# Six probability buffers in place of four, and another written-out order of issue, in a fused attention and feed-forward kernel

## The chip, the cores and the metric

The kernel runs on one core of one Trainium2 chip. The metric is the device time of one execution in microseconds (us), the median of several runs. The engines are called as the profile calls them: PE is TensorE, DVE is VectorE, ACT is ScalarE, POOL is GpSimd, SP is SyncE, whose queue issues every DMA here.

## What is computed

Rotary attention over 4 batches of 8 heads, 576 positions and 64 channels, followed by a feed-forward layer on the 2304 tokens x 512 channels that come out. All in float32.

```python
q_rot, k_rot = (rotate(q), rotate(k))
scores = scale * np.matmul(q_rot, k_rot.transpose(0, 1, 3, 2))
attn = np.exp(scores - np.max(scores, axis=-1, keepdims=True))
attn = attn / (np.sum(attn, axis=-1, keepdims=True) + 1e-09)
x = heads_joined(np.matmul(attn, v))          # 2304 x 512
h = x @ w_in                                   # 2304 x 1024
e = np.exp(h - np.max(h, axis=-1, keepdims=True))
solu = h * (e / (np.sum(e, axis=-1, keepdims=True) + 1e-09))
ln = (solu - solu.mean(-1)) / np.sqrt(solu.var(-1) + 1e-06) * g_ln
return ln @ w_out                              # 2304 x 512
```

## The kernel before, in words

**Attention** goes by 16 pairs of heads, P = 0 to 15, four to a batch. The rotation of a pair's queries and keys is three products and sums for each (line 359), on POOL or DVE. A pair has five score tiles: S P.0 to S P.3 hold 128 rows of each of the two heads, S P.4 packs the last 64 rows of both. PE writes them to PSUM (line 425, the packed ones 452 or 458 and 461), DVE takes the row maxima (405, 472), ACT the exponentials (407, 475) into a probability buffer `e` in SBUF. The buffers are used in turn, tile number j = 5 P + i in buffer j modulo `NE`. Before the values can be applied the tile is transposed: on PE (T steps, line 489, with a copy out of PSUM by ACT, line 328, or DVE, line 330), or, for most tiles of P = 4 and later, by writing it to DRAM (`escr`), reading it back in another order, and a blockwise transpose on DVE (510). Two attention-value blocks per pair (line 564) then add up in PSUM, and DVE scales them into `xT`. From P = 4 on the scores are the sum of three products of split (high and low) operands; the first four pairs use the unsplit ones.

**The feed-forward layer** goes by 18 tiles of 128 tokens. Each of its two matmuls is three products of high and low parts (lines 638 and 711), so 24 matmuls of 512 columns per tile and layer. Between them stand a row maximum (645), an exponential (647), a product (649), a trip through DRAM (`uscr`) with a transpose on DVE (693), and the split into high (`lnh`) and low parts (`lnl`, line 703). The weights arrive as 64-bit words and are decoded in the kernel (tag w, lines 809 to 824: on ACT 809 and 817, on DVE 811, 813 and 818, on POOL 821), in 16 pieces, beside the first four pairs. Before the first scores PE runs a few dummy matmuls (line 725).

**The order of the work** is written out as a list. `Plan.add` numbers 2357 steps as the code builds them, and records each one's engine; `ORDER` is a list of these numbers, and each engine's and each DMA queue's program is the part of the list that belongs to it. Steps with an `alt` may run on a second engine, and do if their number stands in `FLIP`. `BUFS` gives each use of a rotating buffer (three PSUM pairs `D` for scores and hidden rows, two PSUM banks `G`, three SBUF pieces `B`) its place. What must wait for what follows from the data and the buffers; the order itself changes no result.

Numbers that the text speaks of: 118 and 120 are the first two row maxima and 119 and 121 their exponentials; 35, 38, 44 and 47 are decode steps of ACT; 36, 37 and 39 decode steps of DVE; 122 to 125 the first transposes and their copies; 117, 128 and 151 the first three score tiles; 2343 to 2345 the last turn of the last token tile, with its high and low parts.

Of the kernel before, what the change touches and what calls it, by code (L numbers as in the profile page):

```python
# [32 lines left out]
    13, 2, 14, 3, 24, 4, 5, 6, 7, 12, 16, 27, 15, 23, 26, 28, 17, 29, 25, 18, 34, 30, 35, 117, 126, 1, 127,  # L33
    31, 38, 32, 118, 119, 19, 122, 43, 44, 36, 37, 39, 47, 120, 121, 33, 128, 131, 52, 53, 132, 10, 129,
    130, 124, 125, 139, 140, 141, 40, 123, 56, 45, 106, 108, 151, 133, 154, 155, 134, 107, 135, 136, 20,
    114, 61, 152, 153, 142, 109, 46, 48, 110, 62, 115, 65, 112, 160, 163, 137, 138, 161, 164, 158, 159, 143,
    49, 171, 172, 144, 145, 162, 146, 147, 41, 50, 54, 148, 167, 168, 111, 113, 63, 201, 55, 57, 58, 173,
    169, 42, 170, 204, 205, 149, 150, 156, 157, 179, 180, 192, 181, 202, 174, 175, 210, 193, 70, 203, 176,
    178, 64, 165, 177, 166, 116, 206, 207, 213, 214, 208, 209, 79, 186, 211, 194, 182, 185, 195, 71, 233,
    72, 212, 196, 51, 183, 197, 187, 188, 234, 217, 235, 74, 200, 218, 221, 236, 237, 222, 184, 223, 66, 73,  # L40
    67, 59, 224, 60, 80, 242, 243, 215, 68, 216, 199, 245, 246, 189, 190, 75, 238, 239, 81, 191, 76, 253,
    254, 244, 249, 250, 88, 240, 241, 283, 83, 82, 225, 278, 219, 255, 84, 85, 11, 277, 284, 285, 227, 228,
    229, 220, 77, 261, 262, 263, 279, 286, 89, 90, 230, 231, 86, 287, 21, 292, 226, 232, 288, 295, 97, 289,
    251, 296, 252, 258, 293, 294, 247, 248, 315, 69, 260, 98, 301, 302, 78, 259, 275, 318, 319, 446, 87, 99,
    91, 290, 291, 256, 282, 257, 450, 447, 274, 276, 100, 303, 304, 324, 327, 328, 325, 361, 305, 102, 198,
    268, 326, 269, 101, 103, 297, 298, 448, 264, 92, 316, 335, 266, 317, 270, 271, 336, 337, 272, 329, 267,
    330, 362, 265, 93, 104, 373, 363, 273, 364, 94, 320, 321, 340, 342, 374, 375, 299, 300, 105, 449, 341,
    338, 382, 376, 339, 95, 281, 356, 8, 322, 377, 309, 357, 323, 383, 310, 385, 306, 333, 456, 457, 451,
    386, 458, 384, 358, 359, 360, 308, 96, 311, 0, 312, 307, 313, 314, 280, 334, 486, 372, 487, 460, 393,
    394, 405, 395, 343, 378, 379, 488, 380, 344, 381, 406, 407, 345, 368, 22, 459, 461, 371, 9, 391, 396,  # L50
    392, 366, 331, 452, 414, 387, 332, 350, 466, 351, 346, 489, 490, 408, 388, 677, 409, 389, 417, 418, 462,
    415, 416, 398, 425, 463, 365, 453, 693, 491, 492, 676, 390, 397, 426, 427, 678, 696, 476, 697, 399, 400,
    349, 467, 352, 694, 348, 682, 695, 681, 683, 468, 401, 402, 403, 404, 347, 704, 707, 477, 705, 528, 529,
    493, 496, 701, 691, 470, 353, 354, 355, 419, 420, 698, 469, 478, 370, 433, 434, 435, 679, 702, 410, 423,
    424, 534, 471, 472, 706, 479, 412, 413, 692, 481, 436, 369, 454, 708, 530, 709, 531, 430, 494, 431, 495,
    729, 730, 480, 482, 532, 411, 421, 497, 732, 680, 699, 712, 703, 535, 432, 731, 367, 428, 733, 737, 500,
    498, 499, 501, 429, 422, 483, 533, 536, 537, 502, 547, 740, 684, 775, 779, 538, 440, 741, 548, 438, 441,
    780, 539, 717, 718, 742, 437, 710, 743, 442, 439, 506, 700, 503, 719, 713, 734, 443, 744, 715, 716, 752,
    504, 505, 745, 444, 553, 554, 690, 473, 738, 753, 754, 549, 550, 551, 540, 484, 445, 711, 507, 508, 509,
    755, 685, 555, 510, 511, 512, 758, 541, 750, 720, 761, 762, 746, 714, 542, 455, 516, 485, 760, 759, 735,  # L60
    763, 791, 794, 552, 751, 556, 513, 514, 764, 723, 724, 725, 795, 792, 799, 721, 515, 566, 567, 793, 796,
    726, 727, 739, 722, 543, 544, 756, 557, 568, 781, 790, 569, 517, 518, 572, 767, 766, 519, 521, 573, 464,
    574, 575, 520, 558, 559, 757, 522, 765, 474, 475, 736, 465, 686, 523, 524, 525, 802, 803, 804, 687, 748,
    749, 688, 728, 786, 570, 571, 585, 526, 805, 806, 576, 827, 774, 776, 689, 800, 747, 604, 878, 768, 815,
    605, 782, 783, 560, 545, 561, 577, 807, 797, 769, 606, 607, 608, 546, 770, 810, 789, 828, 829, 609, 578,
    562, 563, 771, 772, 816, 817, 808, 622, 832, 527, 579, 777, 778, 830, 831, 835, 610, 838, 839, 811, 841,
    818, 840, 784, 843, 611, 612, 613, 801, 773, 842, 846, 787, 879, 873, 833, 836, 614, 619, 623, 626, 640,
    624, 809, 625, 615, 616, 788, 820, 617, 618, 627, 620, 621, 851, 852, 890, 847, 628, 844, 813, 798, 814,
    629, 819, 630, 631, 893, 880, 853, 854, 889, 632, 881, 812, 894, 874, 891, 892, 895, 633, 634, 564, 901,
    849, 860, 861, 635, 834, 862, 863, 902, 586, 587, 903, 591, 636, 588, 875, 888, 882, 837, 906, 850, 904,  # L70
    905, 644, 855, 856, 898, 885, 926, 886, 848, 565, 637, 845, 866, 927, 876, 909, 857, 859, 858, 581, 896,
    929, 928, 931, 864, 638, 930, 641, 580, 865, 877, 592, 593, 594, 589, 639, 642, 590, 595, 937, 938, 940,
    934, 596, 977, 597, 643, 914, 915, 910, 821, 822, 823, 824, 825, 867, 826, 939, 916, 899, 897, 868, 869,
    870, 871, 645, 785, 941, 872, 907, 949, 932, 950, 912, 913, 988, 911, 951, 976, 978, 952, 991, 883, 646,
    989, 947, 942, 948, 582, 992, 598, 908, 990, 647, 900, 648, 917, 649, 958, 971, 959, 935, 953, 999, 650,
    1000, 651, 954, 972, 973, 974, 960, 987, 979, 583, 584, 933, 1261, 943, 945, 946, 884, 1001, 655, 996,
    1002, 652, 653, 993, 654, 936, 1003, 944, 919, 1024, 1025, 1012, 1013, 1014, 1026, 658, 1027, 656, 920,
    1260, 921, 922, 983, 918, 923, 924, 975, 1028, 1035, 925, 1036, 1038, 1010, 1048, 1011, 955, 1039, 956,
    957, 1037, 659, 980, 1049, 965, 966, 967, 968, 969, 660, 661, 1272, 665, 666, 667, 662, 663, 961, 664,
    668, 669, 1004, 670, 1007, 994, 995, 1050, 1051, 997, 600, 671, 998, 1029, 1015, 1273, 1032, 1262, 1005,  # L80
    963, 887, 1006, 1275, 962, 1008, 964, 970, 1009, 1046, 1030, 1274, 1031, 1040, 1016, 599, 984, 1047,
    1033, 1276, 1283, 601, 1284, 602, 1018, 1019, 1285, 1034, 1043, 1263, 1020, 1021, 1022, 1057, 1017,
    1023, 1070, 986, 1308, 1052, 1286, 1287, 1277, 1041, 1044, 1058, 1071, 657, 672, 1059, 1280, 1278, 1267,
    981, 1288, 1076, 1077, 1291, 1311, 603, 673, 1072, 1073, 1045, 1309, 1312, 1053, 1271, 1042, 1310, 982,
    674, 1265, 1078, 1074, 1075, 1256, 1079, 1296, 1297, 1060, 1279, 1255, 1298, 1257, 1258, 1316, 1054,
    1055, 1056, 1319, 1289, 1294, 1080, 1313, 1081, 1320, 1321, 1270, 1292, 1322, 1264, 1089, 1323, 1064,
    1268, 1065, 1082, 1066, 1259, 1331, 1332, 1370, 1373, 1085, 1295, 1067, 1068, 1358, 1329, 1333, 1334,
    1281, 1090, 1095, 1290, 1091, 1096, 1097, 1299, 1340, 1084, 1371, 985, 1372, 1330, 1314, 1359, 1360,
    1293, 1335, 1324, 1086, 1374, 1336, 1282, 1353, 1354, 1315, 1381, 1337, 1338, 1339, 1365, 1366, 1063,
    1382, 1383, 1384, 1317, 1318, 1385, 1087, 1092, 1093, 1094, 1098, 1341, 1061, 1342, 1300, 1062, 1327,  # L90
    1328, 1069, 1083, 1325, 1266, 1099, 1100, 1394, 1406, 1407, 1108, 1326, 1302, 1303, 1375, 1408, 1355,
    1369, 1301, 1304, 1361, 1362, 1386, 1409, 1305, 1306, 1347, 1109, 1410, 1348, 1395, 1101, 1103, 1356,
    1357, 1165, 1343, 1396, 1307, 1169, 1170, 1349, 1350, 1351, 1417, 1418, 1419, 1368, 1378, 1387, 1166,
    1392, 1167, 1168, 1420, 1458, 1389, 1388, 1171, 1453, 1393, 1110, 1452, 1457, 1376, 1421, 1111, 1112,
    1113, 1114, 1115, 1116, 1117, 1127, 675, 1118, 1102, 1119, 1422, 1377, 1172, 1173, 1088, 1430, 1174,
    1431, 1432, 1411, 1120, 1363, 1345, 1433, 1122, 1123, 1344, 1346, 1352, 1175, 1414, 1176, 1177, 1178,
    1379, 1439, 1440, 1469, 1470, 1471, 1128, 1428, 1180, 1454, 1129, 1429, 1130, 1133, 1183, 1397, 1472,
# [846 lines left out]
```

## Time and profile before

| | us |
|---|---|
| median of 3 runs | 444.42 |
| lowest, highest | 442.26, 445.22 |
| the profiled execution | 442.91 |
| its span, first to last instruction | 441.1 |
| PE, DVE, ACT, POOL busy | 430.2, 377.2, 290.7, 264.4 |

The profile is one execution. Busy time of an engine is the time in which it works on an instruction; for PE the ends of the matmuls are modelled, so neighbours overlap. The profile's lines are those of the kernel's file; a helper's line stands for all its callers (328 and 330 are the two copies, 343 every plain DMA, 359 every product, sum or difference of two tiles).

### The profile page before, as it was taken

The page shows a single profiled execution, that of the slowest core. Times are in us where ns is not written, and L with a number is a line of the kernel's source. Part 1 is how long each engine was busy: PE and PEld are TensorE (multiplying, and loading weights), DVE is VectorE, ACT ScalarE, POOL GpSimd, SP SyncE. Part 2 cuts the span into 40 slices and gives each one's busy share as a digit, 9 for nine tenths or more (in the row PEclk, how much of TensorE's full clock was granted, in tenths as well). Part 3 has the DMA queues.
Part 4 walks back from the last instruction along what each step waited for, and adds up shares of the span by engine and source line. Part 5 has one row for each costly group of instructions (what it writes and reads, how often), then busy time and mean ns, then how long its engine had stood idle before and what let it go on. Part 6 is the DMA issues. An engine that isn't in the chain of part 4 may idle for free.

```text
span 441.1 us, 8137 instructions
## 1 busy us (share of the span) xinstructions
PE 430.2 (98%) x2658; PEld 310.5 (70%) x2658; DVE 377.2 (86%) x601; ACT 290.7 (66%) x644; POOL 264.4 (60%) x295
## 2 busy tenths in 40 slices
PE   7899999999999999999999999999999999999996
PEld 3555656666867776767777778677676776778885
DVE  3899999899999999989889998889889897765663
ACT  1888999999684866767675666675576755335431
POOL 2766767878888585397677868357767320314440
PEclk9999999999999999999999999999999999999999
DMA  7765666879999999998999998899999997434341
GB/s 249 274 207 161 211 176 202 255 230 291 239 319 319 288 297 282 323 305 249 335 320 265 342 268 263 274 298 287 272 310 273 292 303 198 142 121 159 119 144 48
DMA packets 93243, 109.29 MB, mean 248 GB/s; under 512 B 8464, under 2 KB 68752, under 8 KB 93200
## 3 DMA queue, kind: packets, MB, share of 16 engines
q1 hardware_dynamic: 93200, 108.76, 79.1%
q8 instruction: 21, 0.34, 0.3%
q14 instruction: 22, 0.18, 0.1%
HBM read 70.91 MB, written 37.82 MB: 247 GB/s over the span
## 4 chain that ended last, share of the span: by engine, by line
PE 84%; DVE 8%; ACT 3%; DMA 2%; issue 2%; SPq 0%; DVEq 0%; ACTq 0%
PE pg L711 23%; PE pd L638 22%; PE pg L564 16%; PE pd L425 13%; PE pg L489 7%; PE pd L452 2%; DVE mx L405 2%; ACT e L407 1%; DMA rawk<-in_k_t_dram 1%; DMA vst<-in_v_t_dram 1%; DVE xT L818 1%; ACT ET L328 1%; DVE rawq L359 1%; DVE xT L811 1%; ACT xT L809 1%
## 5 line engine op out<-in xcount | busy, mean ns | idle before, releaser
L407 ACT ACTIVATE e<-pd,mx 128x576 f32<-128x576 f32 x132 | 97.7, 742 | 40.6 <-DVE mx L405 24.8
L405 DVE TENSOR_REDUCE mx<-pd 128x1 f32<-128x576 f32 x132 | 95.5, 744 | 13.4 <-PE pd L425 12.3
L510 DVE STREAM_TRANSPOSE ET<-e 128x512 f32<-128x512 f32 x90 | 99.1, 1130 | 0.6 <-DMA e<-escr 0.4
L564 PE MATMUL pg<-ET,vst 128*64 128x320 f32 (+1 forms) x512 | 70.2, 412 | 1.0 <-DVE EL L330 0.8
L703 POOL TENSOR_TENSOR lnl<-tb,lnh 128x512 fp32r<-128x512 f32 x28 | 36.4, 1307 | 50.2 <-ACT lnh L328 35.1
L638 PE MATMUL pd<-wih,xh 128*128 128x512 f32 x144 | 59.2, 411 | 0.0
L711 PE MATMUL pg<-woh,lnh 128*128 128x512 f32 x144 | 58.6, 407 | 0.0
L489 PE MATMUL pg<-idn,e 128*128 128x128 f32 (+1 forms) x308 | 55.0, 296 | 2.6 <-ACT ET L328 1.3
L489 PEld LDWEIGHTS pg<-idn,e 128*128 128x128 f32 (+1 forms) x308 | 40.3, 186 | 23.9 <-issue 7.6
L711 PE MATMUL pg<-woh,lnl 128*128 128x512 f32 x144 | 56.9, 395 | 0.0
L638 PE MATMUL pd<-wih,xl 128*128 128x512 f32 x144 | 56.9, 395 | 0.0
L711 PE MATMUL pg<-wol,lnh 128*128 128x512 f32 x144 | 56.9, 395 | 0.0
L638 PE MATMUL pd<-wil,xh 128*128 128x512 f32 x144 | 56.8, 395 | 0.0
L564 PEld LDWEIGHTS pg<-ET,vst 128*64 128x64 f32 x512 | 33.9, 136 | 25.6 <-issue 3.7
L693 DVE STREAM_TRANSPOSE tb<-wraw 128x512 f32<-128x512 f32 x36 | 39.0, 1113 | 0.9 <-POOL lnl L703 0.8
L359 POOL TENSOR_TENSOR rawk<-rawk,tabs 128x576 f32<-128x576 f32 x24 | 34.2, 1435 | 4.0 <-DMA rawk<-in_k_t_dram 3.9
L359 POOL TENSOR_TENSOR rawq<-rawq,tabs 128x576 f32<-128x576 f32 (+1 forms) x23 | 31.0, 1350 | 9.1 <-DMA rawq<-in_q_t_dram 7.8
L328 ACT COPY ET<-pg 128x512 f32<-128x512 f32 x49 | 27.9, 585 | 12.9 <-PE pg L489 10.4
L359 POOL TENSOR_TENSOR xl<-xT,xh 128x512 fp32r<-128x512 f32 x13 | 16.8, 1294 | 31.4 <-ACT xh L328 30.4
L425 PE MATMUL pd<-kh,qh 64*128 64x288 f32 x192 | 33.3, 343 | 0.3 <-DVE ms L649 0.3
L645 DVE TENSOR_REDUCE ms<-pd 128x1 f32<-128x1024 f32 x18 | 21.9, 1219 | 12.5 <-PE pd L638 12.4
L638 PEld LDWEIGHTS pd<-wih,xh 128*128 128x128 f32 x144 | 27.2, 189 | 6.8 <-ACT e L407 0.8
(122 smaller groups left out, 894.9 us busy)
## 6 DMA issues: line engine op xcount, KB each, us to landing
escr<-e SPq DMA_DIRECT2D x90, 256.0 KB
e<-escr SPq DMA_DIRECT2D x90, 256.0 KB
uscr<-u SPq DMA_DIRECT2D x18, 512.0 KB
wraw<-uscr SPq DMA_DIRECT2D x18, 512.0 KB
rawk<-in_k_t_dram SPq DMA_DIRECT2D x15, 576.0 KB
rawq<-in_q_t_dram SPq DMA_DIRECT2D x15, 576.0 KB
vst<-in_v_t_dram SPq DMA_DIRECT2D x16, 320.0 KB
out_dram<-o SPq DMA_DIRECT2D x18, 256.0 KB
```

Of the source, the lines that this page charges most:

```text
L328: nc.scalar.copy(o, i)
L359: add(*c[0], prio, lambda e: e.tensor_tensor(o, a, b, op=op), r, w, alt=c[1], two=True)
L405: add("dve", 672, t, lambda: nc.vector.tensor_reduce(mx[:, mcol:mcol + 1], buf(us)[:, :, 0:288], axis=AX.XY, op=ALU.max, negate=True), [sk ...
L407: add("act", 720, t, lambda: nc.scalar.activation(e.rearrange("p (z n) -> p z n", z=2), buf(us)[:, :, 0:288], AF.Exp, bias=mx[:, mcol:mcol ...
L425: nc.tensor.matmul(buf(us)[:, z, 0:288], a[rows, c0:c0 + 128], w[rows, 288 * z:288 * z + 288], start=(j == 0), stop=(j == len(terms) - 1))
L489: nc.tensor.transpose(dst, src, idn)
L510: add("dve", 1040, t, lambda: nc.vector.transpose(ET[r][:, h, :, q0:q0 + 128].rearrange("p m (a j) -> p j m a", j=4), e.rearrange("p (j b ...
L564: nc.tensor.matmul(buf(uy)[rows, 0:nq], vv[:, m, h, :], e, start=(m == 0), stop=(m == 4))
L638: nc.tensor.matmul(buf(uh)[:, z, :], a[:, c, :], w[:, c, HF * z:HF * z + HF], start=(c == 0 and j == 0), stop=(c == KC - 1 and j == 2))
L693: add("dve", 1050, tl, lambda z=z, turned=turned: nc.vector.transpose(turned().rearrange("p m (a j) -> p j m a", j=4), v[:, :, 128 * z:128 ...
L703: add(*c[0], tl, lambda e, hd=hd, ld=ld, turned=turned: e.tensor_tensor(ld, turned(), hd, op=ALU.subtract), [bk] + kl[0][z], kl[1][z], use ...
L711: nc.tensor.matmul(buf(uo), a[:, f, :], w[:, f, :], start=(f == 0 and j == 0), stop=(f == FC - 1 and j == 2))
```

## The change

`NE` goes from 4 to 6: two more SBUF buffers of 128 x 1152 float32 for the exponentials. `ORDER`, `FLIP` and `BUFS` are replaced by others, which obey the looser condition that a tile's buffer is read out six tiles later in place of four. The steps themselves, their number (2357), the matmuls, the transfers and which tiles go through DRAM stay. The lists are cut here to their first lines.

```diff
-    13, 2, 14, 3, 24, 4, 5, 6, 7, 12, 16, 27, 15, 23, 26, 28, 17, 29, 25, 18, 34, 30, 35, 117, 126, 1, 127,
-    31, 38, 32, 118, 119, 19, 122, 43, 44, 36, 37, 39, 47, 120, 121, 33, 128, 131, 52, 53, 132, 10, 129,
-    130, 124, 125, 139, 140, 141, 40, 123, 56, 45, 106, 108, 151, 133, 154, 155, 134, 107, 135, 136, 20,
-    114, 61, 152, 153, 142, 109, 46, 48, 110, 62, 115, 65, 112, 160, 163, 137, 138, 161, 164, 158, 159, 143,
-    49, 171, 172, 144, 145, 162, 146, 147, 41, 50, 54, 148, 167, 168, 111, 113, 63, 201, 55, 57, 58, 173,
-    169, 42, 170, 204, 205, 149, 150, 156, 157, 179, 180, 192, 181, 202, 174, 175, 210, 193, 70, 203, 176,
...
+    14, 2, 12, 16, 13, 27, 24, 15, 23, 26, 17, 29, 28, 1, 18, 25, 3, 4, 5, 6, 7, 34, 35, 30, 117, 126, 32,
+    31, 33, 118, 119, 38, 127, 120, 121, 43, 44, 19, 36, 37, 39, 128, 131, 132, 129, 130, 124, 40, 106, 108,
+    122, 123, 139, 140, 141, 9, 125, 151, 154, 133, 47, 109, 135, 152, 155, 45, 46, 134, 110, 136, 48, 49,
+    20, 107, 52, 112, 153, 41, 160, 163, 61, 114, 137, 138, 62, 142, 158, 159, 111, 171, 53, 145, 164, 172,
+    173, 115, 161, 162, 54, 146, 147, 148, 167, 56, 65, 143, 113, 201, 144, 55, 168, 149, 63, 57, 204, 50,
+    58, 169, 150, 170, 179, 192, 205, 174, 156, 210, 175, 157, 70, 193, 194, 176, 180, 181, 202, 203, 42,
...
 FLIP = {
-    23, 24, 25, 33, 42, 45, 72, 77, 78, 96, 112, 113, 125, 138, 194, 195, 196, 197, 216, 220, 252, 259, 260,
-    274, 277, 278, 341, 356, 357, 359, 362, 363, 390, 413, 431, 464, 475, 478, 485, 495, 610, 660, 676, 677,
-    681, 682, 688, 716, 749, 775, 781, 814, 850, 877, 885, 1071, 1089, 1109, 1207, 1363, 1393, 1458, 1558,
-    1649, 1650, 1687, 1781, 1782, 1784, 1881, 1905, 1971, 2173, 2210, 2211, 2270, 2273, 2287, 2291, 2306,
+    23, 25, 33, 42, 45, 51, 72, 90, 96, 108, 110, 112, 113, 159, 178, 193, 195, 196, 197, 216, 259, 260,
+    274, 276, 277, 278, 279, 289, 356, 357, 359, 360, 361, 362, 363, 431, 432, 465, 468, 475, 478, 488, 495,
+    515, 676, 677, 681, 682, 683, 685, 686, 779, 883, 913, 948, 979, 1055, 1056, 1089, 1170, 1171, 1203,
+    1262, 1338, 1356, 1357, 1393, 1460, 1462, 1535, 1552, 1781, 1784, 1798, 1800, 1880, 1881, 1895, 1907,
+    1935, 2172, 2210, 2211, 2249, 2270, 2272, 2287, 2291, 2309, 2326, 2327, 2342, 2344, 2345,
...
 BUFS = (
-    "0021001101001211020111011201010001002010100020100111021100121120101000012100111111201011012111002210"
...
+    "1211020101110100121000101200001000121110210011000200101010020121111011120102110000101020011100110011"
...
     RNG = ((0, 256), (256, 320))
-    NE = 4
+    NE = 6
```

## Rows read from the trace of the kernel before

**Rows 1.** The page, busy time of the engines.
```profile
PE 430.2 (98%) x2658; PEld 310.5 (70%) x2658; DVE 377.2 (86%) x601; ACT 290.7 (66%) x644; POOL 264.4 (60%) x295
```

**Rows 2.** Busy time by stretch, core 0: engine busy (instructions), granted clock, DMA share.
```profile
0.00:15.00 15.00, 12.45 (x33) 5.46 (x34) 7.49 (x13) 4.42 (x8) 4.02 (x16) 1.00 0.84 280
15.00:60.00 45.00, 41.93 (x284) 26.47 (x282) 42.45 (x81) 40.20 (x91) 33.42 (x24) 1.00 0.60 192
60.00:90.00 30.00, 28.71 (x205) 18.85 (x203) 28.22 (x57) 28.54 (x65) 21.18 (x17) 1.00 0.73 229
90.00:130.00 40.00, 39.71 (x252) 28.85 (x251) 38.99 (x65) 34.31 (x75) 34.47 (x34) 1.00 0.90 271
130.00:360.00 230.00, 229.97 (x1526) 171.29 (x1525) 208.59 (x321) 152.20 (x351) 152.25 (x169) 1.00 0.95 292
360.00:441.10 81.10, 77.41 (x372) 59.62 (x371) 51.43 (x69) 31.02 (x59) 19.02 (x38) 1.00 0.44 142
```

**Rows 3.** The chain that ended last: start, length (us), what.
```profile
18.38 1.17 PE pg L489 x8
...
65.12 1.17 PE pd L425 x8
...
150.46 5.00 PE pg L564 x40
...
281.60 0.99 PE pd L425 x12
...
415.01 22.41 PE pg L711 x96
```

**Rows 4.** Timeline from 0 to 22 us: start, length (us), engine, line, operation.
```profile
1.44 7.51 PE L725 MATMUL pg<-lnh 128*128 128x512 f32 x10 [1.44 <-DVE lnh L740]
...
12.62 0.72 ACT L407 ACTIVATE e<-pd,mx 128x576 f32<-128x576 f32 x1
...
14.96 0.74 ACT L407 ACTIVATE e<-pd,mx 128x576 f32<-128x576 f32 x1 [0.40 <-DVE mx L405]
...
17.14 1.24 PE L425 MATMUL pd<-rotk,rotq 64*128 64x288 f32 x8 [0.54 <-ACT e L407]
```

**Rows 5.** Timeline of PE from 140 to 165 us, single matmuls.
```profile
142.37 0.39 PE L638 MATMUL pd<-wih,xl 128*128 128x512 f32 x1
142.60 0.39 PE L711 MATMUL pg<-woh,lnh 128*128 128x512 f32 x1
...
149.07 0.40 PE L638 MATMUL pd<-wih,xl 128*128 128x512 f32 x1
149.40 0.40 PE L425 MATMUL pd<-kh,qh 64*128 64x288 f32 x2
```

**Rows 6.** Waits of ACT: who waited for whom: us, times, longest.
```profile
ACT e L407 <- PE pg L489: 4.0, 3, 2.2
...
ACT e L407 <- DVE ET L510: 2.9, 3, 2.3
```

**Rows 7.** Groups of instructions: count, busy us, mean ns, idle before.
```profile
L359 POOL TENSOR_TENSOR rawk<-rawk,tabs 128x576 f32<-128x576 f32 x24 | 34.2, 1435 | 4.0 <-DMA rawk<-in_k_t_dram 3.9
...
L359 DVE TENSOR_TENSOR rawq<-rawq,tabs 128x576 f32<-128x576 f32 x9 | 6.6, 747 | 0.0
```

**Rows 8.** Timeline from 84.5 to 93 us.
```profile
87.26 1.30 POOL L821 TENSOR_TENSOR xT<-xT,tb 128x512 int32<-128x512 int32 x1
...
87.32 1.53 DVE L813 TENSOR_SCALAR xT<-xT 128x512 uint32<-128x512 uint32 x1 [0.69 <-POOL xT L811]
...
89.50 0.30 PE L489 MATMUL pg<-idn,e 128*64 128x128 f32 x1 [0.48 <-DVE ET L330]
```

**Rows 9.** Line 813 alone: shortest, median and longest ns.
```profile
L813 DVE TENSOR_SCALAR xT<-xT x12: 414/420/1526, 13.1 to 87.3; 128x512 uint32<-128x512 uint32 x12
```

**Rows 10.** The low-part subtraction: its POOL group, and the last one on DVE.
```profile
L703 POOL TENSOR_TENSOR lnl<-tb,lnh 128x512 fp32r<-128x512 f32 x28 | 36.4, 1307 | 50.2 <-ACT lnh L328 35.1
...
432.59 0.68 DVE L703 TENSOR_TENSOR lnl<-tb,lnh 128x512 fp32r<-128x512 f32 x1
```

More of the change, by code (lines that the diff above doesn't have):

```diff
@@ L32 @@
 ORDER = [
[127 rows of a table removed]
[127 rows of a table added]
 ]
 FLIP = {
[5 rows of a table removed]
[5 rows of a table added]
 }
 BUFS = (
-    "0021001101001211020111011201010001002010100020100111021100121120101000012100111111201011012111002210"
-    "0212000211201210112012112011001101200210200001211001010111211010020010120000112210111121001010212202"
-    "1112010020200020011010001021111000220000201002010012011200212010020011020102010112110112101210101101"
-    "02210121121011020200102120000011221001202020000210022110200010201210111"
+    "1211020101110100121000101200001000121110210011000200101010020121111011120102110000101020011100110011"
+    "2020212012111002020110220012001212000201201110200100121201100020101110201111022022120110212002000002"
+    "0002211101011101001221012110001111010111020111110202011020210111201001221202010201011221001002001101"
+    "02200120101211021210121020010101201111020020100221122210010010201120201"
 )
```

243 rows, old and new, of tables (FLIP, ORDER) are left out of this document.

## Prediction

> **What bounds the kernel now.** Read the page's busy line first [rows 1]: TensorE (PE) is busy for 98% of the span, VectorE (DVE) 86%, ScalarE (ACT) 66%, GpSimd (POOL) 60%. An average can hide stages, so the table of windows comes next [rows 2]. It shows three. Up to 15 us PE idles for 2.55 us while the first loads land. From 15 to 90 us DVE and ACT are as full as PE (DVE 42.45 of 45 and 28.22 of 30 us, ACT 40.20 and 28.54), because the weights are decoded there beside the first four head pairs; PE idles 3.07 + 1.29 = 4.36 us. From 90 us PE takes over: 0.29 us idle in 40, then 0.03 us in the 230 up to 360. Of the last window's 3.69 us almost all lies behind the last matmul, which ends at 415.01 + 22.41 = 437.4 [rows 3]. [...]
>
> A busy PE is a modelled figure, so I check it against the chain of work [rows 3]: there each piece lasts until the next begins. the last 96 matmuls of 512 columns take 22.41 us, 0.233 each. Summed over the kernel: 864 of these (18 token tiles x 8 contraction chunks x 3 terms x 2 layers) 201.7 us; 16 pairs of attention-value blocks at 5.00, 80.0; 48 split score tiles at 0.99, 47.5; 16 unsplit ones at 1.17, 18.7; 308 transposes at 1.17 for eight, 45.0; the small rest (sixteen packed score tiles, the column means, the dummies) I put at 24 by the same steps, an estimate. That is 416.9, none of which the change touches. PE works from 1.44 us [rows 4] to 437.4, 436.0 us. So at most 19.1 us are not matmuls, and these contain changes of matmul shape, the wait for the first loads and small hiccups; the idle that the windows show between 15 and 130 us is 4.65 us. Of the two I hold the smaller for what an order of issue can reach, as each stall can hide only 0.40 - 0.23 = 0.17 us behind a modelled end [rows 5].
>
> [...]
>
> **The change part by part.** The sums are made against the profiled execution: 442.91 us, 1.8 above its span of 441.1 and 1.5 below the median 444.42. All runs of before lie within 2.96 us, and 1% is about what a measurement of this kernel can tell from no change.
>
> *Six buffers.* I counted in the two orders: in the new one some 60 of the 160 half-tile exponentials stand ahead of the last reader of the tile four before, which four buffers would forbid; so the room is used. What it can remove is ACT's wait for a buffer to be read out [rows 6]: 4.0 + 2.9 us, six waits. ACT idles for a third of the span and PE for 0.03 us in the stretch where the transposed tiles go through DRAM, so these are worth nothing now. The same longer leads make the stage tolerate later landings, which matters for runs unluckier than this profile; its worth lies between 0 and the 1.5 us by which the median is above the profiled run, and I take 0 of it. The bytes moved and the DMAs are the same in number; the span of SBUF is larger, the transfers are not.
>
> *The first exponentials.* In the old order ACT has two decode steps ahead of the first exponential and two more ahead of the second, and DVE three decode steps between the two row maxima. The exponentials begin at 12.62 and 14.96 us, and the third score tile follows at 17.14 after an idle of 0.54 [rows 4]. In the new order one decode step stands ahead of each, the two maxima are back to back, and the second score tile goes ahead of the first transposes. The first maximum ends where it did; the first exponential can then begin some 0.4 us sooner, and the second after the first (0.74 + 0.19) and one decode step (0.67), near 13.85, 1.1 us sooner. The third score tile needs their PSUM buffers: **-1.1 us**, with ends 0 (the decode steps pushed behind it, 0.7 us each, come back later as waits) and -1.5.
>
> *Fewer changes of shape on PE.* Neighbouring PE steps of different kinds fall from 256 to 248. A score matmul that follows a layer matmul starts 0.33 us after it in place of 0.23 [rows 5], 0.10 us. So -0.8 at most; changes between the two layers cost nothing (again 0.23 from one to the next, same rows), so I take **-0.4**.
>
> *Steps that change their engine.* 22 steps go from POOL to DVE, 20 the other way, and 48, most of them copies and casts, change between ACT and DVE; in all DVE gains 4 steps, POOL loses 2, ACT 2. A rotation product costs 0.75 us on DVE and 1.44 on POOL [rows 7]. Early on the balance is uneven: ahead of the last attention-value block of the second pair DVE's queue holds 15 steps that it did not hold there, less 9 that it did; at the durations of the rows (eight rotation products against one at 0.75, the others at 0.06 to 0.7, an estimate) that is 9.4 - 4.6 = +4.8 us. Five of the 15 belong to later pairs and only stand there early; ahead of the fourth pair's last block the difference is 0.2 us. DVE idles only 2.55 us between 15 and 60 us, so if the five are in the way, PE waits behind row maxima and PSUM copies: between 0 and **+4.8**. I take 0, by the balance at the fourth pair, and because POOL has less ahead there.
>
> *DVE against POOL.* At 87.26 us POOL begins an addition of 1.30 us; at 87.32 DVE begins a shift that takes 1.53 us [rows 8], while the median of that shift is 0.42 [rows 9]; a PSUM copy is queued behind it on DVE, and PE, which waits for that copy, idles 0.48 us before 89.50. [...]
>
> *The rest of the stalls.* Of 4.65 us idle in 15 to 130 us some 1.0 belongs to the first exponentials. The other 3.7 can go wholly, with a few hidden tenths, or stay. DVE and ACT keep their work and are 94 to 95% full there, so I take a quarter: **-0.9**.
>
> *The tail.* The last 96 matmuls run without a gap. The last low-part subtraction moves from DVE (0.68 us, at 432.59) to POOL, where the operation takes 1.31 [rows 10]. Its eight-chunk block starts eight times 0.70 before 437.4, and the half that needs it four times 0.70 before, at 434.6; with the cast ahead of it near 432.7 it ends near 434.0. Cover 0.6 us: **0**, and +0.6 if the cast is that much later. The changed order of the last turns leaves some 0.9.
>
> Sum: -1.1 - 0.4 - 0.9 = -2.4. The profiled execution would go to 440.5, the median to **442.0**, 0.5% less.
>
> **The rivals.**
> *Nothing moves.* The early stage is full on three engines, so what is gained at the start is waited for later; the old stalls come back at other places. For it: DVE 94%, ACT 89 to 95% in those windows. Against it: PE still has idle time that falls on a few steps only. Time: 444.42 - 0.4 = 444.0.
> *The early stalls go.* The longer leads take out the first exponentials' 1.1, the shape changes' 0.8, all of the 3.7, and half of the 1.5 us of late landings: 444.42 - 6.4 = 438.0. Against it: it asks the two full engines to be never late.
> *DVE's early queue is in the way.* The five steps for later pairs and the moved rotation products hold up the row maxima of the second pair, from the point at which more than DVE's 2.55 us of idle in 15 to 60 us is asked for. It costs the whole 4.8 us, and nothing is caught up since PE has no slack behind 90 us: 449.2, over 1% slower.
> *It does not do what it says* is out by the count of the exponentials that run ahead; that the room is worth nothing is in the first rival.
>
> **How the numbers follow.** Forecast (440.0 to 443.5 us): 0.45. Nothing moves (443.5 to 446): 0.27. Early stalls go (below 440.0): 0.22. DVE in the way (above 446): 0.06, of which 0.05 above 448.9. Faster by over 1% means below 440.0: 0.22; slower by over 1%, above 448.9: 0.05; within 1%: 0.73. The range reaches from 438.4, which leaves out half of the third case's better end, to 445.6, where the second case thins out.
>
> **What the profile after would show.** The second exponential near 13.9 us and the third score tile near 16.0 show the first term right; if the third score tile is early and a score tile at 60 us is not, the gain was waited for again. The idle of PE between 15 and 90 us should be near 2.5 to 3.3 us; above 4.4 the second rival holds, and above 7 with DVE releasing PE the last one. ACT's waits for readers of the probability buffers should shrink, without PE's idle between 130 and 360 us changing. The last matmul should run straight on from the layer before it. What would make me wrong most easily: that landings, not the order, set where the median lies above the profiled run.

## The result and the profile after

The changed kernel takes 450.01 us (median of 4 runs, 449.34 to 451.58), the kernel before 443.9 beside it: ratio 1.0144, interval 1.010 to 1.019. It is slower, and by more than the range of the prediction allowed. The profiled execution took 449.34 us, with a span of 447.5.

The page, busy time of the engines, answers to [rows 1].

```profile
PE 427.7 (96%) x2658; PEld 311.4 (70%) x2658; DVE 378.4 (85%) x605; ACT 288.5 (64%) x642; POOL 262.5 (59%) x293
```

The engines have about as much to do as before, in a longer span. Busy time by stretch, as in [rows 2]:

```profile
0.00:15.00 15.00, 11.30 (x36) 5.34 (x37) 7.88 (x15) 4.64 (x8) 3.79 (x14) 1.00 0.82 258
15.00:60.00 45.00, 39.09 (x271) 25.26 (x271) 41.37 (x82) 38.97 (x89) 29.22 (x22) 1.00 0.58 197
60.00:90.00 30.00, 25.83 (x193) 16.79 (x190) 28.03 (x51) 26.70 (x62) 19.85 (x14) 1.00 0.69 208
90.00:130.00 40.00, 40.00 (x246) 29.59 (x244) 36.07 (x58) 35.79 (x77) 30.27 (x28) 0.96 0.83 251
130.00:360.00 230.00, 227.61 (x1504) 170.03 (x1503) 209.98 (x329) 149.54 (x347) 153.07 (x172) 1.00 0.93 293
```

PE's idle from 15 to 90 us is 5.91 + 4.17 = 10.08 us against 4.36 before. DVE idles more too: 3.63 us from 15 to 60 against 2.55. So DVE isn't overfull; it waits, and some of its busy time is steps that take longer than elsewhere (lines below: 1.48 us for a shift whose median is 0.42). From 90 to 130 us the granted clock is 0.96, and two stalls now stand between 130 and 360.

The start is as forecast. The timeline has the first two exponentials and the third score tile [rows 4: 12.62, 14.96, 17.14]:

```profile
12.06 0.74 ACT L407 ACTIVATE e<-pd,mx 128x576 f32<-128x576 f32 x1 [0.21 <-DVE mx L405]
...
13.35 0.73 ACT L407 ACTIVATE e<-pd,mx 128x576 f32<-128x576 f32 x1
...
16.07 1.24 PE L425 MATMUL pd<-rotk,rotq 64*128 64x288 f32 x8 [0.55 <-ACT e L407]
```

To follow lateness further I take the start of a score tile less all PE work issued ahead of it, at one set of durations for both kernels (so another order alone shifts nothing). After less before, in us, by that working (each figure is from one profile, and good to about 0.1):

```
tile            S0.2   S1.4   S2.4   S3.4   S4.2   S5.0   S8.4   S11.2   end
its start (us)   16     41     57     77     93    109    200    266
changed kernel  -1.1   +0.1   +1.1   +1.1   +4.5   +4.6   +5.2   +6.0   +6.4
```

The gain of 1.1 us is gone at 41 us, at 57 it is a loss, and between 77 and 93 us 3.4 us more are lost. What the timeline shows at these three places:

```profile
34.92 2.16 POOL L811 TENSOR_SCALAR xT<-xT 128x512 f32<-128x512 f32 x1 [2.83 <-DMA Rb<-rscr]
...
37.12 0.43 DVE L813 TENSOR_SCALAR xT<-xT 128x512 uint32<-128x512 uint32 x1 [1.05 <-POOL xT L811]
...
39.58 2.08 DVE L405 TENSOR_REDUCE mx<-pd 128x1 f32<-128x576 f32 x3
40.37 0.74 ACT L407 ACTIVATE e<-pd,mx 128x576 f32<-128x576 f32 x1 [1.86 <-DVE mx L405]
...
41.25 0.45 PE L458 MATMUL pd<-rotk,rotq 64*64 64x288 f32 x1 [1.53 <-ACT e L407]
...
51.92 1.40 POOL L359 TENSOR_TENSOR rawk<-rawk,tabs 128x576 f32<-128x576 f32 x1
...
51.95 1.80 DVE L811 TENSOR_SCALAR xT<-xT 128x512 f32<-128x512 f32 x1
...
55.96 1.24 PE L425 MATMUL pd<-rotk,rotq 64*128 64x288 f32 x8 [0.78 <-ACT e L407]
...
84.74 2.15 POOL L811 TENSOR_SCALAR xT<-xT 128x512 f32<-128x512 f32 x1 [1.70 <-ACT xT L809]
...
86.86 1.26 POOL L359 TENSOR_TENSOR xl<-xT,xh 128x512 fp32r<-128x512 f32 x1
86.92 1.48 DVE L813 TENSOR_SCALAR xT<-xT 128x512 uint32<-128x512 uint32 x1 [1.35 <-POOL xT L811]
...
88.32 0.74 DVE L405 TENSOR_REDUCE mx<-pd 128x1 f32<-128x576 f32 x1
88.99 0.47 DVE L569 TENSOR_TENSOR xT<-pg,Rb 128x320 f32<-128x320 f32 x1
...
89.52 0.75 PE L489 MATMUL pg<-idn,e 128*128 128x128 f32 x4 [2.10 <-DVE xT L569]
...
90.35 0.62 PE L638 MATMUL pd<-wil,xh 128*128 128x512 f32 x1
...
90.76 0.63 PE L638 MATMUL pd<-wih,xl 128*128 128x512 f32 x1
...
91.19 0.63 PE L638 MATMUL pd<-wih,xh 128*128 128x512 f32 x1
```

Read the last from its end. PE waits 2.10 us for a PSUM copy (line 569). DVE starts it only at 88.99, since ahead of it in its queue stand a row maximum and a shift of the weight decode (813); the shift waits 1.35 us for its clip (811, step 468), which the new list runs on POOL, 2.15 us, and then takes 1.48 us in place of 0.42 [rows 9], beside a POOL subtraction of 1.26 us that begins 0.06 us before it.

At 41 us it is a shift behind a clip on POOL again, with row maxima queued behind it. But this clip (step 72) is on POOL in the kernel before as well; there two row maxima stand ahead of the shift:

```profile
35.62 2.00 POOL L811 TENSOR_SCALAR xT<-xT 128x512 f32<-128x512 f32 x1 [3.01 <-ACT xT L809]
...
36.30 0.76 DVE L405 TENSOR_REDUCE mx<-pd 128x1 f32<-128x576 f32 x1 [0.45 <-ACT e L407]
...
37.04 0.75 DVE L405 TENSOR_REDUCE mx<-pd 128x1 f32<-128x576 f32 x1
...
39.34 0.41 DVE L813 TENSOR_SCALAR xT<-xT 128x512 uint32<-128x512 uint32 x1
```

So there it is the place in DVE's queue, not a change of engine. At 52 us a clip that is on DVE in both lists (step 99) begins 0.03 us after a rotation product on POOL and takes 1.80 us; the row maxima behind it are late, and PE waits 0.78 us at 55.96.

The matmuls behind the last stall follow each other in 0.41 to 0.43 us, not the 0.233 of [rows 3]. PE stood idle for 2.10 us ahead of them, and narrower windows have the granted clock at 0.50 from 91 to 93 us and at 0.83 from 90 to 100:

```profile
90.00:100.00 10.00, 10.00 (x53) 7.97 (x52) 7.91 (x19) 8.40 (x19) 6.11 (x5) 0.83 0.65 213
```

The view of source line 811 shows what the clip costs on either engine (min/median/max ns), and who waited for it (us, times):

```profile
L811 DVE TENSOR_SCALAR xT<-xT x7: 412/426/1802, 12.6 to 72.8; 128x512 f32<-128x512 f32 x7
L811 POOL TENSOR_SCALAR xT<-xT x5: 1914/2086/2159, 17.8 to 88.1; 128x512 f32<-128x512 f32 x5
...
  DVE xT L813: 3.4, 3
```

Six clips are on POOL (this group and one more): steps 45, 72 and 478, as before, and 90, 468 and 488, which the new list moved. Of the 3.4 us that shifts wait for clips, only the 1.35 at 86.92 is behind a moved one; the others, 0.96 and 1.05, are behind 45 and 72. Late in the run, from 130 to 300 us, PE has two more waits (us, times, longest), which also stand in the windows:

```profile
PE pg L489 <- DVE xT L569: 1.3, 1, 1.3
PE pg L564 <- DMA vst<-in_v_t_dram: 0.9, 1, 0.9
```

### The profile page after: what moved, and what is told of

Same layout as the page of the kernel before. It is cut to its first block, busy times and chain, and to the rows that moved or that the text cites. A ratio compares the mean times of both kernels' runs of the same rounds, so it can differ in the third digit from the quotient of the medians.

```text
span 447.5 us, 8121 instructions
## 1 busy us (share of the span) xinstructions
PE 427.7 (96%) x2658; PEld 311.4 (70%) x2658; DVE 378.4 (85%) x605; ACT 288.5 (64%) x642; POOL 262.5 (59%) x293
## 4 chain that ended last, share of the span: by engine, by line
PE 68%; DMA 14%; DVE 8%; SPq 3%; issue 2%; ACT 2%; POOL 2%; DVEq 0%; ACTq 0%
PE pg L711 19%; PE pd L638 19%; PE pg L564 12%; PE pd L425 9%; PE pg L489 5%; DVE mx L405 3%; DMA uscr<-u 3%; DMA Rb<-rscr 3%; SPq L343 2%; DMA escr<-e 2%; DMA vst<-in_v_t_dram 2%; PE pd L452 2%; DMA e<-escr 1%; DMA rscr<-rs 1%; ACT e L407 1%
## 5 line engine op out<-in xcount | busy, mean ns | idle before, releaser
L405 DVE TENSOR_REDUCE mx<-pd 128x1 f32<-128x576 f32 x132 | 94.3, 743 | 9.5 <-PE pd L425 9.0
L564 PE MATMUL pg<-ET,vst 128*64 128x256 f32 (+1 forms) x512 | 70.0, 412 | 0.9 <-DMA vst<-in_v_t_dram 0.9
L703 POOL TENSOR_TENSOR lnl<-tb,lnh 128x512 fp32r<-128x512 f32 x32 | 41.2, 1291 | 45.3 <-ACT lnh L328 29.0
L489 PE MATMUL pg<-idn,e 128*128 128x128 f32 (+1 forms) x308 | 53.7, 294 | 5.5 <-DVE xT L569 3.7
L359 POOL TENSOR_TENSOR xl<-xT,xh 128x512 fp32r<-128x512 f32 x16 | 21.1, 1317 | 33.1 <-ACT xh L328 13.6
L328 ACT COPY ET<-pg 128x512 f32<-128x512 f32 x51 | 29.2, 588 | 15.2 <-PE pg L489 15.0
L359 POOL TENSOR_TENSOR rawk<-rawk,tabs 128x576 f32<-128x576 f32 x21 | 31.0, 1480 | 2.1 <-DMA rawk<-in_k_t_dram 1.8
L711 PEld LDWEIGHTS pg<-woh,lnh 128*128 128x128 f32 x144 | 27.1, 188 | 7.3 <-issue 1.1
L638 PEld LDWEIGHTS pd<-wih,xl 128*128 128x128 f32 x144 | 27.3, 190 | 6.6
```

Source lines behind the costliest of these rows:

```text
L328: nc.scalar.copy(o, i)
L359: add(*c[0], prio, lambda e: e.tensor_tensor(o, a, b, op=op), r, w, alt=c[1], two=True)
L405: add("dve", 672, t, lambda: nc.vector.tensor_reduce(mx[:, mcol:mcol + 1], buf(us)[:, :, 0:288], axis=AX.XY, op=ALU.max, negate=True), [sk ...
L489: nc.tensor.transpose(dst, src, idn)
L564: nc.tensor.matmul(buf(uy)[rows, 0:nq], vv[:, m, h, :], e, start=(m == 0), stop=(m == 4))
L638: nc.tensor.matmul(buf(uh)[:, z, :], a[:, c, :], w[:, c, HF * z:HF * z + HF], start=(c == 0 and j == 0), stop=(c == KC - 1 and j == 2))
```

## The experiments

My theory: clips moved to POOL, with DVE's next decode step close behind, hold up DVE's queue; late transfers do the rest. Rivals: the buffers; the order of the attention steps; the late part of the list. Each row below is a kernel beside the kernel before on the same chip. The last two columns are the mean granted clock over all executions of each, and an estimate of the loss that it means, in us, (1 - clock) times some 444. It rests on the spell above: from 91 to 93 us, at a granted clock of 0.50, the matmuls lie 0.42 to 0.43 us apart, against 0.23 at 1.00, so near half of the time is lost.

| kernel | us | before | ratio (interval) | clock | loss |
|---|---|---|---|---|---|
| changed kernel, again | 447.97 | 444.15 | 1.0095 (1.006 to 1.013) | 0.9975 | 1.1 |
| before, six buffers | 444.75 | 444.74 | 1.0004 (0.998 to 1.003) | 0.9996 | 0.2 |
| before, the new start | 443.21 | 443.48 | 0.9996 (0.997 to 1.002) | 0.9992 | 0.4 |
| before, three more clips on POOL | 448.16 | 444.74 | 1.0083 (1.005 to 1.012) | 0.9967 | 1.5 |
| before, no clip on POOL | 443.47 | 444.15 | 0.9979 (0.996 to 1.000) | 0.9995 | 0.2 |
| changed, three clips back | 448.64 | 444.74 | 1.0099 (1.007 to 1.013) | 0.9977 | 1.0 |
| changed, no clip on POOL | 446.55 | 443.48 | 1.0081 (1.005 to 1.011) | 0.9954 | 2.0 |
| changed, maxima first | 448.28 | 443.48 | 1.0097 (1.006 to 1.013) | 0.9975 | 1.1 |
| changed, loads sooner (1) | 448.76 | 444.74 | 1.0108 (1.007 to 1.015) | 0.9965 | 1.6 |
| changed, loads sooner (2) | 450.00 | 444.15 | 1.0130 (1.011 to 1.015) | 0.9967 | 1.5 |
| changed, all repairs | 447.42 | 444.15 | 1.0081 (1.006 to 1.011) | 0.9951 | 2.2 |
| changed, old engine list | 485.29 | 443.48 | 1.0900 (1.085 to 1.095) | 0.9707 | 13 |
| new to 105 us, then old | 447.73 | 443.24 | 1.0102 (1.008 to 1.013) | 0.9965 | 1.6 |
| old to 105 us, then new | 444.11 | 443.24 | 1.0006 (0.998 to 1.003) | 0.9990 | 0.4 |
| new to 70 us, then old | 448.06 | 443.36 | 1.0109 (1.008 to 1.014) | 0.9954 | 2.0 |
| old to 70 us, then new | 446.76 | 443.36 | 1.0077 (1.005 to 1.011) | 0.9970 | 1.3 |
| changed, old decode | 475.72 | 443.24 | 1.0714 (1.069 to 1.074) | 0.9684 | 14 |
| before, new decode | 470.15 | 443.24 | 1.0619 (1.059 to 1.065) | 0.9852 | 6.6 |

The kernel before itself has 0.9992 to 0.9997 in its five comparisons. The first four executions of the changed kernel have 0.996, 0.996, 0.992 and 0.996, a loss of 2.2 us on the mean. So by this estimate the clock is a steady part of what the new list costs: 1 to 2 of the 4 to 6 us. It isn't the whole spread: the executions of "the changed kernel again" at 0.999 took 446.08, 446.29 and 449.76 us.

**The changed kernel again.**

> The changed kernel itself, beside the runs that follow. If the order alone sets its time, the ratio is that of the first measurement, 1.0144 (1.010 to 1.019), some 449.5 us; if part of the first figure was the luck of four runs, it lies near the 1.010 that three of its variants had, some 448 us.

447.97: the size is nearer 1.0 than 1.4%. Its profile has the stall of 89.52 again, as long (the same lines of the timeline), but here the matmuls behind it follow in 0.23 us:

```profile
89.43 0.75 PE L489 MATMUL pg<-idn,e 128*128 128x128 f32 x4 [2.10 <-DVE xT L569]
...
90.26 0.39 PE L638 MATMUL pd<-wil,xh 128*128 128x512 f32 x1
...
90.49 0.39 PE L638 MATMUL pd<-wih,xl 128*128 128x512 f32 x1
```

So the stall belongs to the list, the fall of the clock behind it to some executions only (granted clock from 90 to 100 us: 0.83 in the first profile, 1.00 in this one). This profile also lacks the wait of 1.3 us at 256 us: in the first one DVE's scaling ahead of it (line 569) had waited 1.78 us for a DMA to land.

**The buffers, and the start.**

```diff
-    NE = 4
+    NE = 6
```

> The kernel before with six probability buffers and nothing else: its own order, engines and rotating buffers. The clip theory, the late-load theory and the one of DVE's longer front all say that the buffers alone cost and gain nothing: 443.9, within 1 us. Rival, that the buffers themselves cost (another placement in SBUF): above 446.

444.75 against 444.74: more room without a new order is worth nothing and costs nothing. The new start, put into the old list (38, 120, 121, 33 and 128 ahead of 122, 47 and 53 behind it):

```diff
 ORDER:
-    31, 38, 32, 118, 119, 19, 122, 43, 44, 36, 37, 39, 47, 120, 121, 33, 128, 131, 52, 53, 132, 10, 129,
-    130, 124, 125, ...
+    31, 32, 118, 119, 19, 38, 120, 121, 33, 128, 122, 43, 44, 36, 37, 39, 131, 52, 132, 10, 129,
+    130, 47, 53, 124, 125, ...
```

> The kernel before with the changed kernel's start alone: the first two exponentials have one decode step of ACT ahead of each, the first two row maxima are back to back, the second score tile goes ahead of the first transposes. As predicted for this part: the third score tile begins 1.1 us sooner and this stays to the end: 1.1 us under the kernel before. Rival, the decode steps pushed behind come back as waits before 90 us: the same as the kernel before.

443.21 against 443.48, 0.3 us and within the interval: the rival holds, a sooner start is waited for again later.

**The clips.** Three clips of the weight decode go to POOL in the kernel before:

```diff
 FLIP = {
+    90, 468, 488,
```

> The kernel before with only the three clips (steps 90, 468 and 488) on POOL in place of DVE. Clip theory: DVE waits behind them and PE behind DVE, 446 to 448 in place of 443.9, with DVE idle for the clips by 2 us or more (0.7 before). Rival, the longer front of rotation products: DVE is relieved, 443.9 or a little less.

448.16: 3.4 us for three edits of one operation. By the working above it is 0.7 us late at S 2.4 and 3.0 at S 4.2. Its timeline shows both parts of the price:

```profile
87.07 1.50 DVE L813 TENSOR_SCALAR xT<-xT 128x512 uint32<-128x512 uint32 x1 [0.85 <-POOL xT L811]
...
88.25 2.09 POOL L811 TENSOR_SCALAR xT<-xT 128x512 f32<-128x512 f32 x1
...
90.31 1.29 POOL L821 TENSOR_TENSOR xT<-xT,tb 128x512 int32<-128x512 int32 x1
...
90.37 1.51 DVE L813 TENSOR_SCALAR xT<-xT 128x512 uint32<-128x512 uint32 x1 [0.69 <-POOL xT L811]
...
91.81 0.68 DVE L330 COPY ET<-pg 128x512 f32<-128x512 f32 x1
...
92.54 0.30 PE L489 MATMUL pg<-idn,e 128*64 128x128 f32 x1 [1.82 <-DVE ET L330]
```

The shift at 87.07 first waits 0.85 us for its clip (468, moved), then it starts 0.07 us after the next POOL step (87.00, 1.28 us) and takes 1.50 us in place of 0.42. The shift at 90.37 is the one of [rows 8]: it waits behind clip 478, on POOL in both kernels, and its 0.69 and 1.51 us are what it had before (0.69 and 1.53). PE's step behind it, though, now waits 1.82 us for its copy, where it had waited 0.48. The other way round, the kernel before without its own three clips on POOL:

```diff
 FLIP = {
-    45, 72, 478,
```

> The kernel before with its own three clips on POOL (45, 72, 478) moved to DVE. Three more clips on POOL cost 3.4 us. If each clip on POOL costs by itself, some 1.1 us, this gains up to 3 us: 440.5 us. If only those cost that have the next decode step of DVE close behind them, it stays at 443.5 us, or loses up to 1 us because DVE, 94% full there, gets three more steps.

443.47, 0.2% less (interval 0.996 to 1.000): a clip on POOL did not cost by itself there. That it costs where DVE's next decode step stands close behind fits the lines shown; no run varies that distance alone. In the changed kernel the same edit, for the three new ones and then for all six:

```diff
 FLIP = {
-    90, 468, 488,          # the first run
-    45, 72, 90, 468, 478, 488,   # the second
```

> The changed kernel with three clips of the weight decode (steps 90, 468 and 488) back on DVE, as before the change; order, buffers and all else of the change stay. Clip theory: each of them takes about 2.1 us on POOL against 0.42 on DVE, DVE's own queue stands behind it, and PE behind DVE. Then the idle of 2.10 us before 89.5 us and the fall of the granted clock after it (together about 4 us of lag) go, and the median falls from 450.0 to near 446. Rival, the longer front of rotation products in DVE's queue costs the time: DVE only gets more to do, so 450 or more, with the same idle near 89 us.

> The changed kernel with all six clips that it has on POOL (steps 45, 72, 90, 468, 478 and 488) on DVE; order and all else stay. Clip theory: DVE's waits for POOL's clips (3.4 us) go to 0, the idle of 1.5 us before 41.25 us goes as well, so about 2 us less than with three clips moved back: 446.5. Rival, DVE is simply full in this stage and takes 1.3 us more work: 448.6 as with three moved back, or more.

448.64 and 446.55. With three clips back, the wait of 2.10 us becomes two of 0.76 and 0.74, but the time stays 1% above (1.0099), so the 446 that was expected is missed. With all six back the ratio is 1.0081, beside 1.0095 and 1.0144 for the changed kernel: no difference clear of the noise from the second of these. The profile, the fastest execution of twelve, shows less lateness: -1.0 us at S 1.4, 0.0 at S 2.4 and +1.3 at the end (+6.4 and +3.2 in the two profiles of the changed kernel). Over all twelve an estimated 2.0 us are lost to the clock. What is left shows in that profile: the clip is now on DVE, and there it waits itself, for ACT's step ahead of it, with the PSUM copy queued behind:

```profile
82.79 0.43 DVE L811 TENSOR_SCALAR xT<-xT 128x512 f32<-128x512 f32 x1 [1.88 <-ACT xT L809]
...
83.13 1.42 DVE L359 TENSOR_TENSOR rawq<-rawq,tabs 128x576 f32<-128x576 f32 x2
...
84.58 0.76 DVE L359 TENSOR_TENSOR rotq<-rawq 128x576 f32<-128x576 f32 x1
85.26 0.41 DVE L569 TENSOR_TENSOR xT<-pg,Rb 128x256 f32<-128x256 f32 x1
...
85.73 0.75 PE L489 MATMUL pg<-idn,e 128*128 128x128 f32 x4 [0.75 <-DVE xT L569]
```

So the engine of the clip is one part of the matter; the place of the decode step in DVE's queue, ahead of its input, is the other. From S 3.4 to S 4.2 the lateness still grows by 1.4 us here, against 2.4 in the second profile of the changed kernel; the clock is 1.00 in both.

**The engine list, the maxima, the loads.** First the new order with the whole `FLIP` of the kernel before:

```diff
-FLIP = new
+FLIP = old
```

> The changed kernel, its order and six buffers, with every step on the engine that it had before the change (the old list of engine choices). If the engines chosen cost the time (clips and rotation products): 446 or less. If the order costs it: 448.5 to 450 or more, with the same places of idle in the first 90 us.

485.29, far from both expectations. An engine list belongs to its order; this run tells nothing on the cause. Then the row maxima of S 1.2 and S 1.3 (236, 242, 243, 245) ahead of DVE's decode steps:

```diff
 ORDER:
-    ..., 235, 73, 51, ..., 74, 66, 75, ..., 218, 236, 237, 242, 243, ...
+    ..., 235, 236, 73, 51, ..., 74, 242, 243, 245, 66, 75, ..., 218, 237, ...
```

> The changed kernel with three row maxima of the second pair (steps 236, 243 and 245) moved ahead of decode steps in DVE's queue: 236 ahead of the shift that waits for POOL's clip (73), 243 and 245 ahead of steps 66 and 75. Theory of the order in DVE's queue: PE's idle before 41.25 us (1.5 us) goes for the most part and stays gone, -1.2: 448.8. Rival, the engines of this stage are full, and what is gained at 41 us is waited for by 90 us: 450.

The wait at 41.25 went, one of 0.89 us came at 48, and the stall at 89 stayed, 2.11 us: 448.28, no change. The loads of V 7 (887) and of the sums of pair 9 (1443 to 1445) sooner; the first run moved, by a slip of mine, those of pair 10:

```diff
 ORDER:
+    887 ahead of 943, from place 1035 to 948
+    1541, 1543 ahead of 1218          # the first run
+    1443, 1444, 1445 ahead of 1201    # the second
```

> The changed kernel with the load of the eighth pair's values (step 887) moved 87 places forward in the order, to where its buffer is free, and two of the broadcasts of the eleventh pair's reciprocal sums (1541, 1543) moved forward beside the first. Late-load theory: the waits of 0.9 us for the values at 185.9 and of 1.3 us behind the scaling at 256.1 go, so PE idles near 0 from 130 to 360 us in place of 2.39, and the median falls by about 2.2, to 447.8. Rival: the DMA queues are full there (share 0.93), another transfer is late in their place, 450.

> The changed kernel with the load of V 7 issued 87 places sooner and the three loads of the ninth pair's second sums (1443 to 1445) some 50 places sooner, so ahead of two writes to DRAM that stand before them. If these late issues cost what PE's idle at 185.9 (0.9 us) and 256.2 us (1.3 us) shows, the time falls by some 2.0 us against the changed kernel of the same chip, and the idle at 256 us is gone. If the transfers merely queue for something else, or another stall follows, the idle stays or moves and the time with it: 0.

448.76 and 450.00, no gain. In the second the wait at 256 us is gone, while at 187 PE now waits 1.04 us for an exponential where it had waited for V 7. So sooner loads gain nothing. And all repairs together:

> The changed kernel with all three repairs: its six clips of the weight decode on DVE, the row maxima 236, 243 and 245 ahead of decode steps of DVE, and the loads of a_loads2. If the repairs add up (clips -2.5, maxima -0.5, loads -2.0) the time is within 1 us of the kernel before, some 444.5 us. If the rest of the order costs by itself, it stays near the 446.5 us that the clips alone left, 3 us above the kernel before.

447.42: they do not add up. My theory in that form (a few wrong steps, each with its price) fell here.

**Where it is made.** The first part of one list can be joined to the rest of the other: at both places cut, the two beginnings differ by four steps only. Engines and buffers follow the list that a step comes from.

```diff
-ORDER = old
+ORDER = new[:634] + [x for x in old if x not in new[:634]]   # and old first; and 416 in place of 634
```

> The first 634 steps of the new list (to about 105 us, the first four pairs and the decode), then all others as in the kernel before, six buffers. If the loss is made early, this has nearly all of it: 447 to 448 us. If the late loads and the later order make it: 444.5 us.

> The first 634 steps of the list of the kernel before, then all others as in the changed kernel, six buffers. If the loss is made early: 444 to 445.5 us, of which up to 1.5 us are the late landings at 186 and 256 us. If it is made later: 447 us.

447.73 and 444.11. All of the loss is made by the first 634 steps, up to about 105 us; the whole later list, with its late loads and its new last turn, costs 0.1% (interval -0.2 to +0.3). The windows of the run with the old beginning from 15 to 60, 60 to 80 and 80 to 90 us have PE, DVE and ACT within 0.7 us of the kernel before:

```profile
15.00:60.00 45.00, 42.57 (x286) 26.73 (x284) 42.30 (x81) 40.17 (x91) 33.50 (x24) 1.00 0.60 193
60.00:80.00 20.00, 19.20 (x139) 12.60 (x137) 19.32 (x40) 18.85 (x44) 13.78 (x12) 1.00 0.64 200
80.00:90.00 10.00, 9.51 (x68) 6.24 (x66) 8.90 (x18) 9.60 (x22) 7.33 (x6) 1.00 0.92 290
```

> The first 416 steps of the new list (to about 70 us), then all others as in the kernel before, six buffers. The score tiles of the changed kernel stand 1.2 us later than before at 61 to 62 us. If lateness at that point lasts to the end and the stalls near 88 us belong to the second part: 444.5 to 445 us. If the first 70 us also set up the later stalls: 447.5 us. If the second part's order can take it up: 443.5 us.

> The first 416 steps of the list before, then all others as in the changed kernel, six buffers. The run with 634 steps of before ended within 0.1% of it, so what this one loses is made by the steps from 416 to 634, near 70 to 105 us. If the stalls near 88 us and the spell at the lower clock behind them belong to these steps: 446 to 447.5 us. If they only follow from the lateness before them: 444 us.

448.06 and 446.76: each half is enough for most of the loss. In the profile of the second, PE is exactly as late as before up to 78 us (0.0); then the clip (468; of the three moved ones it alone is on POOL in this run), the shift and the copy meet as in the changed kernel, although nothing was late ahead of them:

```profile
83.16 1.99 POOL L811 TENSOR_SCALAR xT<-xT 128x512 f32<-128x512 f32 x1 [2.33 <-ACT xT L809]
...
85.12 1.26 POOL L359 TENSOR_TENSOR xl<-xT,xh 128x512 fp32r<-128x512 f32 x1
85.18 1.48 DVE L813 TENSOR_SCALAR xT<-xT 128x512 uint32<-128x512 uint32 x1 [1.35 <-POOL xT L811]
...
87.25 0.47 DVE L569 TENSOR_TENSOR xT<-pg,Rb 128x320 f32<-128x320 f32 x1
...
87.78 1.13 PE L489 MATMUL pg<-idn,e 128*128 128x128 f32 x4 [2.30 <-DVE xT L569]
```

It is 3.3 us late at S 4.2 (the 2.30, and matmuls 0.43 us apart behind it). This profile is of the slowest of the seven executions, 450.09 us, and 4.0 us more are lost in it between S 5.0 and S 8.4, 1.3 of them in a wait for V values; the median, 446.76, is 3.4 above the kernel before. The first half does it in another way: 0.3 us late at S 1.4 (the clip and the maxima near 41 us), 1.3 at S 2.4 (waits of 0.66 and 0.79 at 52 and 56 us, as in the changed kernel), 2.5 at S 3.4, with no stall of that kind at 89 us (PE busy 9.99 us from 80 to 90), and 4.2 at the end. Added, the two ratios would give 1.0186; the changed kernel had 1.0144 and 1.0095, and the run with the whole new beginning 1.0102. In the lateness of single profiles they come nearer to a sum (2.5 and 2.8 at S 5.0, against 4.6 and 2.9 in the two of the changed kernel), so how far they add stays open.

**The decode alone.** Only the 152 decode steps (tag w) at the old places in the new list, and the reverse:

```diff
-ORDER = new
+ORDER = sorted(steps, key=lambda i: old.index(i) if tag[i] == "w" else new.index(i))   # and old, new exchanged
```

> The changed kernel with only the 152 decode steps of the weights put back: they stand at the places in the list, and run on the engines, that they have in the kernel before; the other 2205 steps keep the new order, engines and buffers among themselves. If the places and engines of the decode steps make DVE wait in front of row maxima and PSUM copies, most of the 4 us go: 444 to 445 us. If the rest of the new order costs by itself (as the 446.6 and 447.4 us that were left without clips on POOL suggest), it stays near 447.5 us.

> The counterpart: the kernel before with only the decode steps at the places and on the engines of the changed kernel, four buffers. If the decode steps are the cause: 447.5 us, with DVE waiting for POOL's clips near 35 and 87 us and PE idle behind it. If the rest of the order is: 444 us.

475.72 and 470.15: neither. Decode steps and attention steps are fitted to each other, so an exchange by the place in the list breaks both; whether the decode or the attention order is "the" cause has no answer of this kind, and stays open.

## Why the prediction was wrong

- **First exponentials, -1.1.** Right in size and place (16.07 against a forecast of 16.0; 13.35 against 13.85), wrong as a term of the sum: the same start in the old list gave 0.3 us, within the noise. It was gone at 41 us, where the chain ran through DVE's queue. I had written this down as the first rival's mechanism and should have put the term there.
- **Steps that change their engine: "I take 0".** This is the step that failed, and the -0.9 for the rest of the stalls failed with it: I held that DVE's new early queue would make PE wait for nothing. PE's idle from 15 to 90 us went from 4.36 to 10.08 us, over the 7 named as the third rival's sign, and the time rose by 3.8 to 6.1 us, all of it made by the first 634 steps. PE is released there by exponentials for 4.8 us and by DVE for 3.7, and ACT's exponentials wait 8.0 us for DVE's row maxima (3.9 before). So that rival had the sign and the place. That its 4.8 us is also near the size is luck, since its mechanism was another: I had counted the busy time of rotation products that go ahead of a block on DVE, and DVE idled more than before. What holds its queue up are decode steps, at three places: one put ahead of row maxima while its input is not ready (41 us), one that runs beside a POOL step (52 us), and one that waits for a clip moved to POOL and then runs beside a POOL step (89 us). For the moved clip I had no price: [rows 7, 10] have sums and products (1.31 to 1.44 us). It stood in the trace of before, by source line:

```profile
L811 DVE TENSOR_SCALAR xT<-xT x9: 413/417/885, 12.2 to 82.3; 128x512 f32<-128x512 f32 x9
...
L811 POOL TENSOR_SCALAR xT<-xT x3: 1928/2003/2120, 15.6 to 85.2; 128x512 f32<-128x512 f32 x3
```

In the old order three such moves measured 3.4 us. In the new order the runs don't show the engines to be the cause: without any clip on POOL the ratio is still 1.0081. What they show is that the first 634 steps, with their engines, are; the share of each place stays open.

- **DVE against POOL: no term.** The forecast names one case [rows 8] and puts no time on such overlaps. Of the 2.10 us at 89.52 about 1.05 is the shift's stretch from 0.42 to 1.48, beside POOL's subtraction, and the clip at 51.95, beside a rotation product on POOL, takes 1.38 us more than the median of before (0.42). Not every overlap is dear: a shift that runs at 74.01 us while POOL works on a clip (73.11 to 75.19) takes 0.41 us. The cost lay in what the list places side by side in front of a copy that PE waits for.
- **The rest of the stalls, -0.9, and the shape changes, -0.4.** The stalls grew by 5.7 us. The shape changes can't be seen behind that, and were not tried by themselves.
- **The clock.** The forecast has no term for it; [rows 2] have 1.00 in every window. In the new list PE's longest stall, 2.10 us, is followed by a granted clock of 0.83 from 90 to 100 us in the first profile of the changed kernel, and of 1.00 in the second. Over all its executions the clock column means an estimated 1 to 2 us on the mean.
- **Six buffers, 0; the tail, 0.** Right: 1.0004 for the buffers alone, 1.0006 for everything behind 105 us.

## What to carry to other kernels

In a list where one engine's queue serves both a pipeline of decode steps and the copies that the bottleneck waits for, price a moved step by who stands behind its consumer, not by its busy time: three clips of 2 us on an engine that was idle for 40% of the span cost 3.4 us. Price its place in the queue in the same way: a step whose input isn't ready holds up all behind it, on whichever engine the input is made. Look up the duration of each moved operation on its new engine; "elementwise on POOL" was 1.3 us for one operation and 2.1 for another of the same shape. And this finely fitted order wasn't mended by moving back single steps (no repair gained anything clear of the noise, nor did all together), but it could be cut in time: first part of one, rest of the other told within two runs where the loss was made.

## What the runs showed of the hardware

In the traces of the two kernels the one-input clip of 128x512 float32 (line 811) took 1.91 to 2.16 us on POOL, and the two-input integer sum of the same shape (line 821) 1.28 to 1.74 us there. On DVE the median of the clip was 0.42 us before the change and 0.43 after it.

Of the 32 shifts in these two traces (line 813, all on DVE), five began with 0.28 us or more of a two-input POOL step (lines 359 and 821) to go, and took 0.58, 0.71, 0.83, 1.48 and 1.53 us. The other 27 took 0.41 to 0.46 us, among them the one at 74.01 us in the changed kernel, beside a one-input clip on POOL.

In both profiles of the changed kernel PE stood idle for 2.10 us until DVE's line 569 was done, near 89.5 us. The next layer matmuls (line 638) ran 0.41 to 0.43 us apart in the first and 0.23 in the second, with a granted clock of 0.83 and of 1.00 from 90 to 100 us.
